# Crossing the moving columns of the split products, storing every second partition, and a new order of work from step 32 on

## The chip, the cores and the metric

The kernel runs on one core of a Trainium2 chip. A core has TensorE (PE, products of matrices), VectorE (DVE), ScalarE (ACT), GpSimd (POOL) and SyncE (SP, which here issues the transfers). Each works through its own list of instructions in order, and they wait for one another by semaphores. Operands lie in SBUF, on 128 partitions; products land in PSUM. The metric is the time on the device in microseconds (us), as a median over timed runs.

## What is computed

A retention layer (attention with a decay in place of the softmax) is followed by a feed-forward layer whose activation is a quotient of polynomials. From the reference, cut to what matters:

```python
scores = scale * np.matmul(q, k.transpose(0, 1, 3, 2))      # 8 x 8 heads, 576 x 64
ret = scores * Dmat[None, :, :, :]                          # Dmat = gamma ** (i - j), lower triangle
x = np.matmul(ret, v)                                       # as tokens: 4608 x 512
h = x @ w_in                                                # 512 x 2048
P = a[0] + a[1] * h + a[2] * h2 + a[3] * h3
Q = 1.0 + np.abs(b[0]) * np.abs(h) + np.abs(b[1]) * h2
g = P / (Q + 1e-06)
return (g @ w_out).astype(np.float32)                       # 2048 x 512
```

## The kernel before

The tokens are worked on in 9 blocks of 512 (`b`), and the 2048 inner columns in 16 slices of 128 (`f`). One step is one pair (b, f), 144 steps in all. The feed-forward part of a step is:

- `gemm1`: the first product, h = w_in slice x tokens, 128 partitions of inner columns by 512 tokens. To keep precision in the fast format fp32r, both factors are split into a rounded part and a rest (`xhi`, `xlo`; `w[:, 0]`, `w[:, 1]`), and three products are added up: 4 pieces of 128 x 3 = 12 products that each stream 512 columns of x.
- `ffn_p`, `ffn_p2`, `ffn_va`, `ffn_v`, `ffn_r`, `ffn_q`, `ffn_q3`: the activation on ScalarE and VectorE. ScalarE makes p and u from `h` (a2 + a3 h and |h|), later v from u, and the reciprocal of v as a logarithm and an exponential, both written into u. VectorE does `p*h`, `p2`, `v*u`, and after the reciprocal `p*u`, `v*u+..` and the last product p. `ffn_r`, `ffn_q` and `ffn_q3` of a step run one step later.
- `ffn_hi`, `ffn_lo`: the split of the result into `g[:, 0]` and `g[:, 1]`, two steps later.
- `gemm2`: the second product, three or four steps later. For each quarter t of the block (128 tokens), three products stream the 512 columns of w_out's slice and add to `acc`; 12 products a step. With the block's last slice, `acc` is copied to `o` and stored.

In the first part of the program, four slices of w_out aren't split yet when they are wanted; there `gemm2` takes one product in plain fp32 with the tile `held` (called `plain[f]` in the code), four a step, 16 in all.

The retention part is done in units of 128 tokens. A `visit` on PE takes 64x64 products for one unit's outputs (`ps`) and the next unit's scores and state (`y`, `ps`); `decay`, `add`, `keep_hi`, `keep_lo` and others bring them through VectorE, ScalarE and GpSimd. From step 30 on a visit comes every fourth step, the last at step 126.

The order of work within a step is written by hand: `run` goes through a list of names. Steps 0 to 31 have lists of their own (`FIRST..`, `MID`, `DENSE..`); all steps from 32 on use `REST`, and the last ones without a first product use `END`. The list sets the order on each engine, since every instruction is kept in program order. Transfers are all issued by SP, in the order in which the code comes to them: weights early, one unit's q, k and v after each visit, and the stores.

The tiles u and v have two buffers each, p three, and the tile `h` in PSUM two (one of which a visit takes for `y`).

Of the kernel before, what the change touches and what calls it, by code (L numbers as in the profile page):

```python
# [12 lines left out]
F32 = mybir.dt.float32  # L13
# [4 lines left out]
AF = mybir.ActivationFunctionType  # L18
ALU = mybir.AluOpType
PSUM = bass.MemoryType.PSUM  # L20

P = 128
B, H, S, D = 8, 8, 576, 64
NT = B * S
DM = H * D
DFF = 2048
NPAIR = H // 2
NU = NT // P
NB = NT // 512
NF = DFF // P  # L30
# [19 lines left out]
DENSE = "scale_q gemm1 visit decay ffn_p split0 ffn_hi split1 ffn_va ffn_r gemm2 ffn_lo keep_hi ffn_v ffn_p2 split2 split3 scale_v ffn_q ffn_q3 decay1 add keep_lo fade".split()  # L50
DENSE_ALONE = "gemm1 ffn_r ffn_p visit decay decay1 ffn_p2 ffn_q keep_hi split2 ffn_va add scale_v ffn_hi split3 ffn_v fade scale_q gemm2 split0 ffn_lo keep_lo ffn_q3 split1".split()
REST = (
    "gemm1 ffn_p visit ffn_p2 ffn_hi decay keep_hi ffn_lo decay1 add fade keep_lo scale_q scale_v ffn_va ffn_v gemm2 ffn_r"
    " ffn_q ffn_q3"
).split()
END = "ffn_r ffn_hi gemm2 ffn_lo ffn_q ffn_q3".split()

# [31 lines left out]
def retention_ffn(ctx: ExitStack, tc: tile.TileContext, qkv, w_in, w_out, consts, masks, out):  # L89
# [10 lines left out]
    nc = tc.nc  # L100
# [6 lines left out]
    cnv = ctx.enter_context(tc.tile_pool(name="cnv", bufs=4))  # L107
# [8 lines left out]
    pe, act, dve, pool = (InOrder(tc, e) for e in (nc.tensor, nc.scalar, nc.vector, nc.gpsimd))  # L116
# [43 lines left out]
    plain, held = {}, []  # L160
# [309 lines left out]
    part = []  # L470
    spare = {}

    def gemm1(b, f):
        xhi, xlo = xs[b]
        w = parts[0, f]
        h = hs[b, f] = ps_h.tile([P, 512], F32, tag="h", name=f"h{b}_{f}")
        for c in range(NPAIR):
            cs = slice(c * P, (c + 1) * P)
            for k, (j, x) in enumerate(((0, xhi), (0, xlo), (1, xhi))):
                pe.matmul(  # L480
                    h, w[:, j, cs], x[:, c, :], start=(c == 0 and k == 0), stop=(c == NPAIR - 1 and k == 2)
                )

    def ffn_p(b, f):
# [56 lines left out]
    def is_plain(b, f):  # L541
        return at[b, f] < half and str(f) in PLAIN
# [17 lines left out]
    def acc_of(b, t):  # L560
        return accs[b][2][:, 0, :] if b == NB - 1 and t == 3 else accs[b][t // 2][:, t % 2, :]

    def gemm2(b, f, first, last):
        if first:
            accs[b] = [ps_acc.tile([P, 2, DM], F32, tag="acc", name=f"acc{b}_{f}_{t}") for t in range(2)]
            if b == NB - 1:
                accs[b].append(ps_at.tile([P, 2, DM], F32, tag="at", name=f"acc{b}_{f}_2"))
        g = gs.pop((b, f))
        if is_plain(b, f):
            for t in range(4):  # L570
                pe.matmul(acc_of(b, t), g[:, t * P : (t + 1) * P], plain[f], start=first, stop=last)
            return
        w = parts[1, f]
        for t in range(4):
            ts = slice(t * P, (t + 1) * P)
            acc = acc_of(b, t)
            for k, (i, j) in enumerate(((0, 0), (0, 1), (1, 0))):
                pe.matmul(acc, g[:, i, ts], w[:, j, :], start=(first and k == 0), stop=(last and k == 2))
        if not last:
            return  # L580
        if b == NB - 1:
            for t in range(4):
                r0 = b * 512 + t * P
                o = cnv.tile([P, DM], F32, tag="c", name=f"o{b}_{t}")
                if t == 1:
                    dve.tensor_scalar(o, acc_of(b, t), -1.0, None, ALU.mult)
                else:
                    act.activation(o, acc_of(b, t), AF.Copy, scale=-1.0)
                nc.sync.dma_start(out[r0 : r0 + P, :], o)
            return  # L590
        for t, acc in enumerate(accs.pop(b)):
            r0 = b * 512 + t * 256
            rows = out[r0 : r0 + 256, :].rearrange("(t p) d -> p t d", p=P)
            if b == 1:
                for j in range(2):
                    o = cnv.tile([P, DM], F32, tag="c", name=f"o{b}_{t}_{j}")
                    act.activation(o, acc[:, j, :], AF.Copy, scale=-1.0)
                    nc.sync.dma_start(rows[:, j, :], o)
                continue
            if b == 0 and f == NF - 1:  # L600
                o = part[t]
                dve.scalar_tensor_tensor(o, acc, -1.0, o, ALU.mult, ALU.add)
            else:
                o = op.tile([P, 2, DM], F32, tag=f"o{t}", name=f"o{b}_{t}_{f}")
                act.activation(o, acc, AF.Copy, scale=-1.0)
            if f < NF - 1:
                part.append(o)
            else:
                nc.sync.dma_start(rows, o)

# [1 line left out]
    first = half + NF  # L614
# [81 lines left out]
    def products(i):  # L696
        nonlocal done
        while done < len(steps) and i - done >= lag(i):
            gemm2(*steps[done])
            done += 1  # L700

    for i in range(len(steps) + lag(len(steps))):
# [4 lines left out]
        if i in VISITS:  # L707
            a, k = VISITS[i]
# [63 lines left out]
```

## Time and profile before

| what | value |
|---|---|
| time, median of 3 runs | 894.04 us (893.99 to 895.55) |
| span of the profiled execution | 891.7 us |
| median less the span | 2.3 us |
| PE busy | 879.0 us, 99% |
| VectorE busy | 792.2 us, 89% |
| ScalarE busy | 674.3 us, 76% |
| GpSimd busy | 124.6 us, 14% |

The span runs from the first to the last instruction of one execution. The time of a run is a little longer, as it holds what lies around the span. A busy share is an average over the whole span, so it does not say which engine is waited for in a given stretch.

### The profile page before, as it was taken

The page shows a single profiled execution, that of the slowest core. Times are in us where ns is not written, and L with a number is a line of the kernel's source. Part 1 is how long each engine was busy: PE and PEld are TensorE (multiplying, and loading weights), DVE is VectorE, ACT ScalarE, POOL GpSimd, SP SyncE. Part 2 cuts the span into 40 slices and gives each one's busy share as a digit, 9 for nine tenths or more (in the row PEclk, how much of TensorE's full clock was granted, in tenths as well). Part 3 has the DMA queues.
Part 4 walks back from the last instruction along what each step waited for, and adds up shares of the span by engine and source line. Part 5 has one row for each costly group of instructions (what it writes and reads, how often), then busy time and mean ns, then how long its engine had stood idle before and what let it go on. Part 6 is the DMA issues. An engine that isn't in the chain of part 4 may idle for free.

```text
span 891.7 us, 18668 instructions
## 1 busy us (share of the span) xinstructions
PE 879.0 (99%) x7574; PEld 721.0 (81%) x7574; DVE 792.2 (89%) x1222; ACT 674.3 (76%) x1239; POOL 124.6 (14%) x107
## 2 busy tenths in 40 slices
PE   8899999999999999999999999999999999999998
PEld 6667888888888888888888888888888888888886
DVE  5999999998899888898999988888888989888895
ACT  4889998986677787777777787778777787667774
POOL 3424325421101100010111110111000111000000
PEclk9999999999999999999999999999999999999999
DMA  9993000141211112011211131112111021001001
GB/s 343 344 381 134 1 1 1 49 143 49 96 48 49 49 49 77 28 40 48 96 48 49 48 96 49 48 49 96 48 37 31 31 95 49 1 1 47 1 1 47
DMA packets 20454, 64.55 MB, mean 72 GB/s; under 512 B 2192, under 2 KB 2320, under 8 KB 20368
## 3 DMA queue, kind: packets, MB, share of 16 engines
q1 hardware_dynamic: 20368, 63.36, 20.2%
q8 instruction: 59, 0.97, 0.4%
q14 instruction: 27, 0.22, 0.1%
HBM read 53.91 MB, written 9.44 MB: 71 GB/s over the span
## 4 chain that ended last, share of the span: by engine, by line
PE 91%; DVE 5%; DMA 2%; ACT 1%; issue 1%; SPq 0%; DVEq 0%
PE acc L85 43%; PE h L85 41%; PE ps L85 4%; PE y L85 2%; DVE p L85 2%; DMA bits<-in_w_out 2%; PE psNone L85 1%; DVE v L85 1%; DMA qk<-in_qkv 1%; DVE qk L85 0%; DVE xlo L85 0%; DVE kv L85 0%; DVE c L85 0%; ACT o L85 0%; PE ps_None L85 0%
## 5 line engine op out<-in xcount | busy, mean ns | idle before, releaser
L85 PE MATMUL acc<-w,g 128*128 128x512 f32 x1584 | 384.3, 392 | 0.6 <-ACT o L85 0.3
L85 PE MATMUL h<-xhi,w 128*128 128x512 f32 x1152 | 378.9, 390 | 0.7 <-DVE kv L85 0.7
L85 PEld LDWEIGHTS acc<-w,g 128*128 128x128 f32 x1584 | 294.9, 188 | 63.6 <-ACT o L85 0.7
L85 PEld LDWEIGHTS h<-xhi,w 128*128 128x128 f32 x1152 | 216.3, 188 | 47.1 <-ACT u L85 1.0
L85 PE MATMUL h<-xlo,w 128*128 128x512 f32 x576 | 224.2, 389 | 0.1
L85 ACT ACTIVATE p<-h,const_sb 128x512 f32<-128x512 f32 x144 | 111.7, 776 | 127.8 <-PE h L85 123.6
L85 DVE SCALAR_TENSOR_TENSOR p<-p,const_sb,u 128x512 f32<-128x512 f32 x131 | 117.7, 899 | 15.6 <-ACT u L85 15.6
L85 PEld LDWEIGHTS h<-xlo,w 128*128 128x128 f32 x576 | 108.1, 188 | 23.4 <-issue 0.7
L85 DVE TENSOR_TENSOR p<-p,h 128x512 f32<-128x512 f32 x144 | 98.8, 686 | 28.1 <-ACT u L85 27.8
L85 DVE TENSOR_TENSOR v<-v,u 128x512 f32<-128x512 f32 x131 | 96.0, 733 | 24.8 <-ACT v L85 24.8
L85 ACT ACTIVATE u<-h 128x512 f32<-128x512 f32 x131 | 77.9, 594 | 48.0 <-DVE v L85 46.5
L85 DVE SCALAR_TENSOR_TENSOR p<-p,const_sb,h 128x512 f32<-128x512 f32 x144 | 107.6, 748 | 4.8
L85 ACT ACTIVATE v<-u,absb 128x512 f32<-128x512 f32 x129 | 103.9, 806 | 0.3 <-DVE p L85 0.2
L85 DVE SCALAR_TENSOR_TENSOR p<-v,p 128x512 f32<-128x512 f32 x140 | 97.5, 697 | 4.1
L85 DVE SCALAR_TENSOR_TENSOR v<-v,u 128x512 f32<-128x512 f32 x131 | 91.7, 700 | 0.0
L85 ACT ACTIVATE g<-p 128x512 fp32r<-128x512 f32 x132 | 83.3, 631 | 8.3 <-DVE p L85 3.4
L85 POOL TENSOR_TENSOR S<-S,const_sb 128x256 f32<-128x256 f32 x32 | 21.1, 659 | 472.6 <-DVE S L85 470.0
L85 ACT ACTIVATE u<-u 128x512 f32<-128x512 f32 x131 | 82.9, 633 | 4.2
L85 ACT ACTIVATE u<-v 128x512 f32<-128x512 f32 x131 | 81.3, 621 | 1.5 <-DVE v L85 1.5
L85 DVE TENSOR_TENSOR g<-p,g 128x512 fp32r<-128x512 f32 x115 | 78.7, 684 | 1.4 <-ACT g L85 1.4
L85 ACT ACTIVATE kv<-kv,const_sb 128x64 f32<-128x64 f32 x232 | 58.4, 339 | 4.8 <-DMA kv<-in_qkv 4.8
L85 POOL TENSOR_TENSOR qk<-qk,const_sb 128x512 f32<-128x512 f32 x31 | 48.4, 1562 | 47.5 <-DMA qk<-in_qkv 47.2
(93 smaller groups left out, 691.5 us busy)
## 6 DMA issues: line engine op xcount, KB each, us to landing
qk<-in_qkv SPq DMA_DIRECT2D x36, 512.0 KB, 4.0
kv<-in_qkv SPq DMA_DIRECT2D x32, 512.0 KB, 5.4
bits<-in_w_in SPq DMA_DIRECT2D x16, 512.0 KB, 9.5
bits<-in_w_out SPq DMA_DIRECT2D x16, 512.0 KB, 7.7
out<-o SPq DMA_DIRECT2D x14, 512.0 KB, 4.4
out<-o SPq DMA_DIRECT2D x8, 256.0 KB, 2.7
kv<-in_qkv SPq DMA_DIRECT2D x4, 256.0 KB, 6.8
const_sb<-in_consts SPq DMA_DIRECT2D x1, 265.0 KB, 3.1
```

The lines of the kernel that those rows point to most:

```text
L85: return lambda *a, **k: self.tc.keep_in_program_order(method(*a, **k))
```

## The change

All split products read their moving operand through `crossed`: column 0 of the first half, column 0 of the second half, column 1 of the first half and so on. The order of the 512 streamed columns is thereby changed, so the columns of `h`, `g` and the sums stand for other tokens: partition p of a sum's quarter t is token a x 256 + t x 64 + p // 2 with a = p % 2. Each store is therefore cut in two, one for the even and one for the odd partitions (`o[a::2]`). The columns of w_out are put in the opposite order on the host, so that the output's columns come out as they were; the `held` products read theirs crossed too. The list `REST` is new. A few lines of the diff that only change a tile's shape are cut.

```diff
 REST = (
-    "gemm1 ffn_p visit ffn_p2 ffn_hi decay keep_hi ffn_lo decay1 add fade keep_lo scale_q scale_v ffn_va ffn_v gemm2 ffn_r"
-    " ffn_q ffn_q3"
+    "gemm1 visit decay ffn_p scale_q decay1 ffn_p2 ffn_hi ffn_r ffn_va scale_v keep_hi ffn_lo ffn_q keep_lo add"
+    " ffn_q3 fade gemm2 ffn_v"
 ).split()
...
+    def crossed(x):
+        return x.rearrange("p (a n) -> p n a", a=2)
+
...
-                    h, w[:, j, cs], x[:, c, :], start=(c == 0 and k == 0), stop=(c == NPAIR - 1 and k == 2)
+                    h, w[:, j, cs], crossed(x[:, c, :]), start=(c == 0 and k == 0), stop=(c == NPAIR - 1 and k == 2)
...
-                pe.matmul(acc_of(b, t), g[:, t * P : (t + 1) * P], plain[f], start=first, stop=last)
+                pe.matmul(acc_of(b, t), g[:, t * P : (t + 1) * P], crossed(plain[f]), start=first, stop=last)
...
-                pe.matmul(acc, g[:, i, ts], w[:, j, :], start=(first and k == 0), stop=(last and k == 2))
+                pe.matmul(acc, g[:, i, ts], crossed(w[:, j, :]), start=(first and k == 0), stop=(last and k == 2))
...
-                nc.sync.dma_start(out[r0 : r0 + P, :], o)
+                store(b, t, o)
...
-                nc.sync.dma_start(rows, o)
+                store(b, 2 * t, o)
+
+    def store(b, t, o):
+
+        n = o.shape[1]
+        for a in range(2):
+            r0 = b * 512 + a * 256 + t * D
+            nc.sync.dma_start(out[r0 : r0 + n * D, :].rearrange("(t m) d -> m t d", m=D), o[a::2])
...
+    w_out = moe_w_out.reshape(DFF, DM // 2, 2).transpose(0, 2, 1)
...
-        "w_out": np.ascontiguousarray(moe_w_out).view(np.int64).reshape(NF, P, DM),
+        "w_out": np.ascontiguousarray(w_out).view(np.int64).reshape(NF, P, DM),
```

The order of the rows on PE and GpSimd is the same before and after, apart from the numbers in the names. The next two pairs show VectorE and ScalarE in one visit step from 32 on; the first number in a name is the slice f, the last one only tells buffers apart.

VectorE before, from slice 6's `p*h` (first row) to slice 5's last product; `qk`, `kv`, `S` and `xlo` are the visit's rows:

```order
L85 TENSOR_TENSOR p_6_3964<-p_6_3964,h_6_3949 128x512
L85 SCALAR_TENSOR_TENSOR p_6_3964<-p_6_3964,const_sb,h_6_3949 128x512
L85 TENSOR_TENSOR qk_3772<-y_3969,mask_sb 128x256
L85 COPY kv_3774<-y_3969 128x256
L85 TENSOR_TENSOR g_4_4041<-p_4_3871,g_4_4041 128x512
L85 TENSOR_TENSOR qk_3772<-ps_18_3968,mask_sb 128x256
L85 TENSOR_TENSOR S_4048<-kv_3774,ps_18_3968 128x256
L85 TENSOR_TENSOR xlo_3782<-ps_18_3968,xhi_3781 128x4x128
L85 TENSOR_TENSOR v_6_3963<-v_6_3963,u_6_3962 128x512
L85 SCALAR_TENSOR_TENSOR p_5_3913<-p_5_3913,const_sb,u_5_3911 128x512
L85 SCALAR_TENSOR_TENSOR v_5_3912<-v_5_3912,u_5_3911 128x512
L85 SCALAR_TENSOR_TENSOR p_5_3913<-v_5_3912,p_5_3913 128x512
```

VectorE after, the same step:

```order
L85 TENSOR_TENSOR qk_3772<-y_3971,mask_sb 128x256
L85 COPY kv_3774<-y_3971 128x256
L85 TENSOR_TENSOR p_6_4046<-p_6_4046,h_6_3957 128x512
L85 TENSOR_TENSOR qk_3772<-ps_18_3970,mask_sb 128x256
L85 SCALAR_TENSOR_TENSOR p_6_4046<-p_6_4046,const_sb,h_6_3957 128x512
L85 TENSOR_TENSOR g_4_4052<-p_4_3879,g_4_4052 128x512
L85 SCALAR_TENSOR_TENSOR p_5_3921<-p_5_3921,const_sb,u_5_3919 128x512
L85 SCALAR_TENSOR_TENSOR v_5_3920<-v_5_3920,u_5_3919 128x512
L85 TENSOR_TENSOR xlo_3792<-ps_18_3970,xhi_3791 128x4x128
L85 TENSOR_TENSOR S_4062<-kv_3774,ps_18_3970 128x256
L85 SCALAR_TENSOR_TENSOR p_5_3921<-v_5_3920,p_5_3921 128x512
L85 TENSOR_TENSOR v_6_4045<-v_6_4045,u_6_4044 128x512
```

The step's own `v*u` (v_6) has moved behind the two readers of the previous slice's reciprocal (u_5) and is now last; the rows that read `y` have moved ahead of `p*h`.

ScalarE before, the same step; u_5<-v_5 and u_5<-u_5 are the logarithm and the exponential:

```order
L85 ACTIVATE p_6_3964<-h_6_3949,const_sb 128x512
L85 ACTIVATE u_6_3962<-h_6_3949 128x512
L85 ACTIVATE g_4_4041<-p_4_3871 128x512
L85 ACTIVATE xhi_3781<-ps_18_3968 128x4x128
L85 ACTIVATE v_6_3963<-u_6_3962,absb 128x512
L85 ACTIVATE u_5_3911<-v_5_3912 128x512
L85 ACTIVATE u_5_3911<-u_5_3911 128x512
```

ScalarE after, from slice 4's g (the rows p_6 and u_6 stand ahead of it as before):

```order
L85 ACTIVATE g_4_4052<-p_4_3879 128x512
L85 ACTIVATE u_5_3919<-v_5_3920 128x512
L85 ACTIVATE u_5_3919<-u_5_3919 128x512
L85 ACTIVATE v_6_4045<-u_6_4044,absb 128x512
L85 ACTIVATE xhi_3791<-ps_18_3970 128x4x128
```

The logarithm and exponential of slice 5 have moved ahead of slice 6's v and of the visit's `xhi`.

SP's last rows before, the stores of the last block:

```order
L609 DMA out<-o_0_15_8771 128x2x512
L609 DMA out<-o_1_15_8774 128x2x512
L589 DMA out<-o_0_9374 128x512
L589 DMA out<-o_1_9377 128x512
L589 DMA out<-o_2_9380 128x512
L589 DMA out<-o_3_9383 128x512
```

And after:

```order
L616 DMA out<-o_0_15_8791 64x2x512 x2
L616 DMA out<-o_1_15_8795 64x2x512 x2
L616 DMA out<-o_0_9392 64x512 x2
L616 DMA out<-o_1_9396 64x512 x2
L616 DMA out<-o_2_9400 64x512 x2
L616 DMA out<-o_3_9404 64x512 x2
```

Each store has become two of half the partitions, issued one after the other in the same place.

## Rows read from the trace of the kernel before

**Rows 1.** The page: span, busy time of PE, clock in 40 slices.

```profile
span 891.7 us, 18668 instructions
...
PE 879.0 (99%) x7574; PEld 721.0 (81%) x7574; DVE 792.2 (89%) x1222; ACT 674.3 (76%) x1239; POOL 124.6 (14%) x107
...
PEclk9999999999999999999999999999999999999999
```

**Rows 2.** Chain that ended last, 860 to 892 us: start, length, what.

```profile
860.18 2.72 PE h L85 x12
...
873.78 13.61 PE acc L85 x60
```

**Rows 3.** Stretches: length, busy PE, PEld, DVE, ACT, POOL, clock, DMA share, GB/s.

```profile
25.61:216.94 191.33, 188.59 (x1697) 149.43 (x1693) 183.63 (x292) 168.57 (x313) 66.96 (x52) 1.00 0.33 121
75.68:94.72 19.04, 19.04 (x86) 15.77 (x84) 18.93 (x31) 17.36 (x31) 7.48 (x6) 1.00 0.02 9
385.10:409.12 24.02, 24.02 (x226) 19.90 (x224) 21.80 (x34) 17.68 (x34) 2.22 (x2) 1.00 0.14 45
768.59:792.02 23.43, 23.31 (x162) 19.06 (x160) 18.99 (x30) 15.05 (x26) 0.00 (x0) 1.00 0.00 1
792.02:813.78 21.76, 21.76 (x98) 18.02 (x96) 17.64 (x28) 15.50 (x25) 0.00 (x0) 1.00 0.13 49
```

**Rows 4.** Groups by shape, PE: count, busy us, mean ns.

```profile
L85 PE MATMUL acc<-w,g 128*128 128x512 f32 x1584 | 384.3, 392 | 0.6 <-ACT o L85 0.3 <-DVE o L85 0.3
L85 PE MATMUL h<-xhi,w 128*128 128x512 f32 x1152 | 378.9, 390 | 0.7 <-DVE kv L85 0.7
L85 PE MATMUL h<-xlo,w 128*128 128x512 f32 x576 | 224.2, 389 | 0.1
...
L85 PE MATMUL acc<-w,spare 128*128 128x512 f32 x96 | 22.7, 389 | 0.0
```

**Rows 5.** Timeline of PE at 59 us: start, length of the run of eight.

```profile
58.95 3.59 PE L85 MATMUL acc<-held,g 128*128 128x512 f32 x8
```

**Rows 6.** The tile `held`, weight loads (PEld) and products: shortest, median and longest ns.

```profile
L85 PEld LDWEIGHTS acc<-held,g x32: 186/190/190, 40.9 to 69.3; 128*128 128x128 f32 x32
L85 PE MATMUL acc<-held,g x32: 590/592/697, 40.9 to 69.8; 128*128 128x512 f32 x32
```

**Rows 7.** Groups of VectorE and ScalarE, 216.94 to 862.60 us (645.66 us).

```profile
L85 ACT ACTIVATE p<-h,const_sb 128x512 f32<-128x512 f32 x109 | 84.7, 777 | 112.2 <-PE h L85 110.7 <-DVE v L85 1.4
L85 DVE SCALAR_TENSOR_TENSOR p<-p,const_sb,h 128x512 f32<-128x512 f32 x110 | 82.3, 748 | 3.9
L85 DVE TENSOR_TENSOR v<-v,u 128x512 f32<-128x512 f32 x110 | 77.7, 707 | 24.6 <-ACT v L85 24.6
L85 DVE SCALAR_TENSOR_TENSOR v<-v,u 128x512 f32<-128x512 f32 x110 | 77.3, 703 | 0.0
...
L85 DVE TENSOR_TENSOR p<-p,h 128x512 f32<-128x512 f32 x109 | 75.0, 688 | 23.2 <-ACT u L85 23.0
L85 DVE TENSOR_TENSOR g<-p,g 128x512 fp32r<-128x512 f32 x105 | 71.8, 684 | 0.0
L85 ACT ACTIVATE u<-u 128x512 f32<-128x512 f32 x109 | 69.0, 633 | 3.5
L85 ACT ACTIVATE u<-v 128x512 f32<-128x512 f32 x109 | 67.6, 620 | 0.0
L85 ACT ACTIVATE g<-p 128x512 fp32r<-128x512 f32 x105 | 66.4, 633 | 4.6
L85 ACT ACTIVATE u<-h 128x512 f32<-128x512 f32 x109 | 64.9, 596 | 47.0 <-DVE v L85 45.6
```

**Rows 8.** The output tensor: the last four stores' issues, ns.

```profile
L589 SPq DMA_DIRECT2D out<-o x4: 344/378/413, 886.7 to 888.3; - x4
```

**Rows 9.** What SP waited for: us in total, times, longest.

```profile
SPq L377 <- PE ps L85: 633.4, 59, 98.8
```

**Rows 10.** The page's transfers: KB each, median us from issue to landing.

```profile
qk<-in_qkv SPq DMA_DIRECT2D x36, 512.0 KB, 4.0
```

## What I expect, and why

> **What bounds the kernel now.** I read the page first: in a span of 891.7 us TensorE (PE) is busy 99%, and its granted clock is at the upper level, 2.4 GHz, in every slice [rows 1]. Then the chain that ended last: near its end it shows PE's big products in unbroken runs, 12 in 2.72 us and 60 in 13.61 us [rows 2]. That is 226.7 ns from one product to the next. A product streams 512 columns, and at 2.4 GHz one column a cycle would take 213.3 ns; 13.4 ns of each product are something else. The groups by shape count 1584 + 1152 + 576 + 96 = 3408 such split products [rows 4], 772.6 us at this pace, 87% of the span.
>
> The table of stretches says where PE alone sets the pace. A period of four steps with one visit takes 24.02 us and PE is busy in all of it; four steps without a visit take 21.76 us, which is 96 x 226.7 ns to the last digit [rows 3]. In the early part it is different: from 75.68 to 94.72 VectorE (DVE) works 18.93 of 19.04 us, as full as PE [rows 3].
>
> One other kind of product in this trace streams 512 columns of four-byte numbers: those with `held`, kept in plain fp32. The code asks for 16 and the records show 32, so each is two passes. Eight passes in a row take 3.59 us, the last one's 592 ns among them [rows 5, 6], so one follows the other after (3.59 - 0.592) / 7 = 0.4283 us. That is 1024 cycles at 2.4 GHz (426.7 ns) and 1.6 ns more: a column every second cycle, with next to nothing on top. The same bytes lose 1.6 ns at half the pace and 13.4 ns at the full pace.
>
> **The change: crossed columns.** The products, their count and PE's order stay; only the addresses of the moving columns change: 0, 256, 1, 257 and so on, two places 1 KB apart, each read at half the pace. No row shows such a stream, so I bound it. From below 213.3 + 1.6 = 214.9 ns a product, if the loss is that one place doesn't deliver a column in every cycle; from above 428.3 ns, a column every second cycle, the pace of the `held` row. Between them lies 226.7, no effect. I take 215.2 ns, a saving of 11.5 ns, near the lower end: the loss goes with the full pace of one stream, `held` reads one place at half pace and loses almost nothing, and each of the two places is now read at just that pace. Waiting for weights it is not: `held` has loads of the same 128 x 128 shape, 190 ns each, without the loss [rows 6], and 190 ns is less than the product that a load lies under.
>
> The Trainium skill, "TensorE: Matmul & The Clock Gate", section "Wait — 56ns, not 53.3ns?", gives 215.7 ns from one warm 512-column product to the next. The split products here don't reach it (226.7 ns); by its figure the saving would be 11.0 ns, an estimate, and the sum some 1.4 us smaller.
>
> **What of it reaches the end.** From 216.94 us on (step 32) there are 112 x 12 first products and 115 x 12 second ones, which run three steps behind: 2724 x 11.5 ns = 31.3 us. A period falls from 24.02 to 24.02 - 96 x 0.0115 = 22.92 us. VectorE has 21.80 us of work in it [rows 3], so it still fits, with 1.1 us to spare where it had 2.2. Some of what it waits for now is only PE's pace, handed on by ScalarE as `u` (23.0 us ahead of `p*h` in this stretch); but 24.6 us are waits for ScalarE's `v` [rows 7], 24.6 / (645.66 / 24.02) = 0.9 us a period, and ScalarE's `u` waits 45.6 us for VectorE's `v` [rows 7]: the two hand work back and forth.
>
> *The new order* changes ScalarE's and VectorE's rows from step 32 on. Before, a step's `v*u` stands on VectorE ahead of the previous step's two readers of the reciprocal, which queue behind its wait; now it is the last row of the step, and ScalarE does logarithm and exponential ahead of `v`. By durations, from `h` ready: ScalarE's p 0.78, u 0.60, g 0.63, logarithm 0.62, exponential 0.63 end at 3.26 us; VectorE, behind `u` (1.38), does `p*h`, `p2` and `g`, 0.69 + 0.75 + 0.68, until 3.50 us [rows 7], so the reciprocal is there when it is wanted. The buffer that the next `u` needs is free after two more rows, 3.50 + 0.75 + 0.70 = 4.95 us, ahead of the next `h` at 24 x 0.2152 = 5.16 us. So the 0.9 us go. What remains is unevenness: each visit puts some 21.80 - 17.64 = 4.2 us more work for VectorE into one step of four [rows 3], against 24.02 - 21.76 = 2.26 us for PE; VectorE falls behind by some 1.2 us and has three steps with 0.7 us to spare each to make it up, while PE has a second buffer for `h`. For the 24 visits I allow 0.12 us each, 2.9 us (none at all, or the 0.9 us kept without cover, 21.80 + 0.9 = 22.7, would still be under 22.92). 31.3 - 2.9 = 28.4 us.
>
> *Before step 32* there are 684 products, 7.9 us at most; VectorE leaves 191.33 - 183.63 = 7.7 us idle there in all, and stretches like 75.68 to 94.72, where it leaves 0.11 us, give nothing [rows 3]. I take a quarter of the 7.9, 1.9 us.
>
> *Stores.* Each becomes two of 64 partitions on SP's queue, 22 issues to 44, at 378 ns the median one of the last four [rows 8]. In the middle SP waits 633 us on the visits alone [rows 9], and the loads behind a store land in 4.0 us [rows 10] and are scaled three steps, some 16 us, later; that cover makes the extra issues free, and without it they would cost 22 x 0.378 = 8.3 us. At the end nothing covers them: the second half of the last store is issued 0.38 us later, with half the bytes in each: +0.3 us.
>
> *Sum.* On the profiled execution 891.7 - 28.4 - 1.9 + 0.3 = 861.7 us. The median of the timed runs, 894.04, lies 2.3 us above that span, so 864 us.
>
> **The rivals.** *VectorE takes up what PE gives.* If all its 2.2 us of waits in a period stay, because ScalarE and VectorE hand work back and forth as before, a period with a visit stays at 24.0, and only the steps without visits, from 768.59 us on [rows 3], gain (some 516 products, 5.9 us) with the 1.9 us early: 886. For it: VectorE is busy 91% of a period. Against it: the timing of the new order above. A loss of which half is removed (220.9 ns) gives much the same: 894 - 15 - 1 = 878.
>
> *The excess belongs to the product, not to the addresses*: a fixed turn between products that shows only when the stream is short. Nothing excludes it, as all split products have one length. Then only the order and the tail move: 893 to 895, since PE is full anyway.
>
> *The other side: jumping is dearer than running on.* One mechanism: a column whose neighbour isn't read right after it needs a fetch of its own, and the stream waits for it. At worst a product goes to 428.3 ns: 3408 x 201.6 ns = 687 us more, 1581 us. It decides from 0.5 ns a product on (1.8 us over 3408). For it: no moving operand in this trace jumps, so nothing shows that a jump is free. Against it: at half the pace each place has the time that it has in `held`.
>
> The Trainium skill, "SBUF — State Buffer", section "Door 1: The DMA port swizzle (why `[64,N]` ≈ `[32,N]`)", speaks for this rival: lines of 16 bytes, of which at least two accesses in a row are wanted, and a penalty for each step to a new line. By it a product makes 512 line changes where it makes 128 now; if the 11.8 ns are the price of 128, four times that gives 262 ns a product and about 1013 us, an estimate. No row of this trace shows it.
>
> **How the numbers follow.** Loss gone and VectorE keeping up: 0.50, 857 to 873 us. Loss gone in part, or VectorE in the way: 0.14, 873 to 892. No effect: 0.13, 892.3 to 895.8 (0.2%, 1.8 us, is about what a measurement of this kernel can tell from no change). Slower: 0.23, nearly all of it above 900, since any real price is paid 3408 times. The prediction is the first case, 864, and its own range 857 to 873. The whole range, 856 to 898, holds the first three cases and leaves out the slower one. Faster 0.64, same 0.13, slower 0.23.
>
> **What would show it.** Right: twelve split products in 2.58 us in the chain, periods of 22.9 to 23.1 us, VectorE busy 93% or more in them, `v` no longer waiting for ScalarE, 0.3 us more behind the last product. Wrong: a pace of 226.7 (the excess is the product's own), one above it (jumps cost), or the new pace with periods still near 24 (VectorE). The prediction stands or falls with the pace of one product, on which the trace before has only the `held` row to say.

## The result and the profile after

The changed kernel takes 873.31 us (median of 4 runs, 873.01 to 874.14) against 894.01: a ratio of 0.9766, 95% interval 0.9752 to 0.978. That is 20.7 us less where 30 were forecast. The profiled execution has a span of 871.7 us, 1.6 less than the median (2.3 before).

The page first, its span and its busy times [rows 1 for before]:

```profile
span 871.7 us, 18740 instructions
PE 851.0 (98%) x7574; PEld 727.6 (83%) x7574; DVE 774.6 (89%) x1222; ACT 664.8 (76%) x1239; POOL 131.5 (15%) x107
```

PE has lost 28.0 us of busy time, the span 20.0. So 8 us of what the products gave went elsewhere. The chain that ended last shows the pace itself and what stands behind the last first product (start, length, what):

```profile
842.73 2.59 PE h L85 x12
845.32 2.59 PE acc L85 x12
847.91 2.60 PE h L85 x12
...
861.10 0.64 ACT g L85
861.74 0.04 issue
861.78 0.70 PE acc L85 x2
862.50 2.44 PE acc L85 x10
864.95 0.02 issue
864.97 0.60 ACT o L85
```

Twelve products take 2.59 us where they took 2.72 [rows 2]: 215.9 ns each, 10.8 less. The stretches are steps 0 to 31, a part of them, one period with a visit, four steps without one, and step 32 to the end of the last first product (length, busy PE, PEld, DVE, ACT, POOL, clock, DMA share, GB/s):

```profile
28.00:222.93 194.93, 185.89 (x1696) 149.76 (x1693) 187.63 (x292) 174.93 (x313) 66.60 (x52) 1.00 0.32 114
98.49:121.11 22.62, 20.98 (x97) 18.06 (x96) 22.09 (x34) 21.52 (x35) 6.97 (x6) 1.00 0.00 1
383.93:406.87 22.94, 22.94 (x225) 20.02 (x224) 20.53 (x34) 16.82 (x34) 2.60 (x2) 1.00 0.14 47
772.64:793.36 20.72, 20.72 (x97) 18.14 (x96) 18.17 (x29) 16.09 (x26) 0.00 (x0) 1.00 0.08 32
...
222.93:850.34 627.41, 626.65 (x5497) 546.36 (x5496) 562.40 (x894) 468.47 (x887) 54.46 (x42) 1.00 0.15 50
```

A period has gone from 24.02 to 22.94 us and PE is still busy in all of it [rows 3]. Steps 0 to 31 have got longer, 191.33 to 194.93 us, with VectorE's busy time up from 183.63 to 187.63. In four parts, with the borders at the first product of step 0, at that of step 32, and where the product behind the last first one starts (850.34 us):

| part | before | after | moved | forecast |
|---|---|---|---|---|
| ahead of step 0 | 25.61 | 28.00 | +2.4 | 0 |
| steps 0 to 31 | 191.33 | 194.93 | +3.6 | -1.9 |
| step 32 to the last first product | 656.7 | 627.4 | -29.3 | -28.4 |
| behind it | 18.1 | 21.4 | +3.3 | +0.3 |
| span | 891.7 | 871.7 | -20.0 | -30.0 |

The large part came out about as forecast; the three small ones all went the wrong way. The groups of VectorE and ScalarE from 222.93 to 842.73 us answer to [rows 7] (count, busy us, mean ns, idle before):

```profile
L85 ACT ACTIVATE p<-h,const_sb 128x512 f32<-128x512 f32 x110 | 85.2, 775 | 150.9 <-PE h L85 148.1 <-DVE g L85 2.7
...
L85 DVE TENSOR_TENSOR v<-v,u 128x512 f32<-128x512 f32 x110 | 83.1, 756 | 0.0
...
L85 DVE TENSOR_TENSOR p<-p,h 128x512 f32<-128x512 f32 x110 | 75.4, 685 | 36.9 <-ACT u L85 35.0
...
L85 ACT ACTIVATE u<-h 128x512 f32<-128x512 f32 x110 | 64.3, 585 | 1.0 <-DVE v L85 0.9
```

The wait for `v` (24.6 us) is gone, and so is `u`'s wait for VectorE's `v` (45.6, now 0.9). What VectorE still waits for, `u`, is PE's pace handed on: ahead of its p, the row that comes before `u`, ScalarE waits 148.1 us for PE's `h`.

For steps 0 to 31 two tiles tell more. `held`, the plain fp32 products [rows 6], and `bits`, the weight words that ScalarE and VectorE bring into fp32 (shortest, median and longest ns):

```profile
L85 PE MATMUL acc<-held,g x32: 701/703/804, 43.6 to 74.6; 128*128 128x512 f32 x32
...
L85 ACT ACTIVATE bits<-bits x32: 654/870/980, 20.6 to 175.7; 128x512 int32<-128x512 uint32 x32
L85 ACT ACTIVATE c<-bits x28: 655/862/910, 20.0 to 175.2; 128x512 f32<-128x512 f32 x28
L85 DVE SCALAR_TENSOR_TENSOR c<-c,bits x28: 679/835/1955, 21.7 to 178.9; 128x512 int32<-128x512 int32 x28
```

The kernel before has for the last three:

```profile
L85 ACT ACTIVATE bits<-bits x32: 648/668/691, 18.5 to 168.0; 128x512 int32<-128x512 uint32 x32
L85 ACT ACTIVATE c<-bits x28: 649/661/689, 17.9 to 167.4; 128x512 f32<-128x512 f32 x28
L85 DVE SCALAR_TENSOR_TENSOR c<-c,bits x28: 678/684/1782, 19.6 to 171.1; 128x512 int32<-128x512 int32 x28
```

Nobody touched these rows, and their medians rose by 150 to 200 ns. All read every second four-byte word of a tile; rows that read neighbours, like VectorE's g<-p with 684, kept their length in these steps. The `held` passes rose from 592 to 703 ns. Both are taken up in the experiments.

At the end the timeline of SP has the last stores (start, length of all, the line, count), after and before:

```profile
864.29 4.98 SPq L616 DMA_DIRECT2D out<-o  x8
```

```profile
886.68 2.08 SPq L589 DMA_DIRECT2D out<-o  x4
```

One issue of a store of every second partition takes 608 ns at the median, not 378 [rows 8]. From the end of PE's last product to the end of the span it is now 871.7 - 864.94 = 6.8 us, before 4.3 (PE ended at 873.78 + 13.61 = 887.39): 2.5 of the 3.3 us. The other 0.8 lie between the last first product and PE's last second one, 14.6 us against 13.8: before, PE ran its 60 last products without a break [rows 2]; now the chain there goes through the last step's activation and its `g`, which didn't get faster.

Ahead of step 0, PE's timeline (start, length, what, count):

```profile
8.68 1.12 PE L85 MATMUL unread<-whole_sb,qk 128*128 128x128 f32 x4
...
11.53 1.12 PE L85 MATMUL unread<-whole_sb,qk 128*128 128x128 f32 x4
...
16.08 0.66 PE L85 MATMUL unread<-whole_sb,qk 128*128 128x128 f32 x4
```

Four such products take 1.12 us twice and then 0.66; before, those at 10.03 us took 0.66 already. The change moves nothing there. In the profiled executions of the experiments step 0 began at 25.39 to 26.56 us in eight and at 28.96 and 29.23 in two (x_crossed and early_less). In x_crossed the granted clock is 0.50, the lower of its two levels (1.2 GHz), near 13 us, behind a wait of PE of 1.59 us at 9.34. In early_less such products take 1.12 us at 9.17 and 12.28 us and 0.66 at 17.32, and there the granted clock shows it, in the windows view from 8 to 18 us:

```profile
8.00:18.00 10.00, 7.81 (x78) 6.21 (x78) 4.19 (x8) 3.69 (x11) 2.70 (x3) 0.66 1.03 411
```

That is 0.66 of 2.4 GHz as a mean, between the lower and the upper level, behind PE's wait of 1.83 us at 9.17. For the changed kernel's own profile the view reads 1.00 in that window, but its trace holds no record of the clock ahead of 14.05 us, and the view counts such time as full; in the other eleven profiles the record begins between 3.9 and 6.6 us. The products fit the lower level up to there: 1.12 us at 11.53 us, 0.66 at 16.08. So a granted clock that rose late in this execution is the likely cause, though no record of the lower level shows it. The 2.4 us belong to the execution; how much of them is in the medians stays open. This bears on every comparison with this profile: a part of the difference of two spans can lie ahead of step 0, so the parts of the span are given where they matter.

### The profile page after: what moved, and what is told of

It is laid out like the page before. It is cut to its first block, busy times and chain, and to the rows that moved or that the text cites. A ratio compares the mean times of both kernels' runs of the same rounds, so it can differ in the third digit from the quotient of the medians.

```text
span 871.7 us, 18740 instructions
## 1 busy us (share of the span) xinstructions
PE 851.0 (98%) x7574; PEld 727.6 (83%) x7574; DVE 774.6 (89%) x1222; ACT 664.8 (76%) x1239; POOL 131.5 (15%) x107
## 4 chain that ended last, share of the span: by engine, by line
PE 81%; DVE 11%; ACT 4%; issue 2%; DMA 1%; POOL 0%; SPq 0%; ACTq 0%; DVEq 0%; POOLq 0%
PE acc L85 37%; PE h L85 36%; DVE p L85 5%; PE ps L85 4%; DVE v L85 3%; PE y L85 2%; DVE c L85 1%; PE psNone L85 1%; ACT free_at L85 1%; ACT g L85 1%; DMA qk<-in_qkv 1%; DVE qk L85 0%; ACT bits L85 0%; ACT c L85 0%; ACT u L85 0%
## 5 line engine op out<-in xcount | busy, mean ns | idle before, releaser
L85 PE MATMUL h<-xhi,w 128*128 128x512 f32 x1152 | 367.8, 381 | 3.9 <-DVE p L85 3.2
L85 PE MATMUL acc<-w,g 128*128 128x512 f32 x1584 | 367.8, 381 | 3.4 <-ACT o L85 1.6
L85 PE MATMUL h<-xlo,w 128*128 128x512 f32 x576 | 218.4, 379 | 0.1
L85 DVE TENSOR_TENSOR v<-v,u 128x512 f32<-128x512 f32 x131 | 101.4, 774 | 0.2 <-ACT v L85 0.2
L85 DVE SCALAR_TENSOR_TENSOR p<-p,const_sb,u 128x512 f32<-128x512 f32 x131 | 99.3, 758 | 1.2 <-ACT u L85 1.2
L85 POOL TENSOR_TENSOR S<-S,const_sb 128x256 f32<-128x256 f32 x32 | 27.1, 848 | 454.9 <-DVE S L85 454.9
L85 DVE SCALAR_TENSOR_TENSOR v<-v,u 128x512 f32<-128x512 f32 x131 | 89.4, 683 | 0.0
```

The source lines that it names most:

```text
L85: return lambda *a, **k: self.tc.keep_in_program_order(method(*a, **k))
```

## Experiments

The medians of before beside these runs are 893.7 to 893.9 us. Ratios are against before, with 95% intervals.

**cross_only: the crossed columns with the old order.**

```diff
 REST = (
-    "gemm1 visit decay ffn_p scale_q decay1 ffn_p2 ffn_hi ffn_r ffn_va scale_v keep_hi ffn_lo ffn_q keep_lo add"
-    " ffn_q3 fade gemm2 ffn_v"
+    "gemm1 ffn_p visit ffn_p2 ffn_hi decay keep_hi ffn_lo decay1 add fade keep_lo scale_q scale_v ffn_va ffn_v gemm2 ffn_r"
+    " ffn_q ffn_q3"
 ).split()
```

> The change with the old list REST from step 32 on. Theory: the pace of one product does all the work and the order little, because even with the 0.9 us of waits for ScalarE's v kept in a period VectorE needs 21.8 + 0.9 = 22.7 us, less than PE's 22.94; periods stay at 22.9 to 23.1 us and the time at 872 to 876 us. Rival: the old order hands work back and forth between ScalarE and VectorE and can't follow the shorter step; periods of 23.3 to 24.0 us, 24 of them, 882 to 893 us.

884.51 us (883.53 to 885.35), 0.989 (0.9874 to 0.9907): 11.2 us slower than the change. In the profiled executions the part from step 32 to the last first product is 13.7 us longer. Its window of one period, and its waits from 246 to 760 us (us in total, times, longest):

```profile
410.32:433.96 23.64, 23.34 (x225) 19.86 (x224) 21.45 (x34) 19.31 (x35) 2.30 (x2) 1.00 0.25 89
```

```profile
ACT u L85 <- DVE v L85: 85.8, 85, 2.3
DVE v L85 <- ACT v L85: 27.1, 22, 1.2
...
PEld h L85 <- DVE p L85: 14.2, 20, 1.0
...
PE h L85 <- DVE p L85: 6.0, 18, 0.6
```

The old order holds a period at 23.64 us, and PE now waits for VectorE's `p`, the reader that gives `h` free, though VectorE is busy for only 21.45 of it. The two engines hand work back and forth, and that chain binds before either is full.

**order_only: the kernel before with the new order.** The same list the other way round:

```diff
 REST = (
-    "gemm1 ffn_p visit ffn_p2 ffn_hi decay keep_hi ffn_lo decay1 add fade keep_lo scale_q scale_v ffn_va ffn_v gemm2 ffn_r"
-    " ffn_q ffn_q3"
+    "gemm1 visit decay ffn_p scale_q decay1 ffn_p2 ffn_hi ffn_r ffn_va scale_v keep_hi ffn_lo ffn_q keep_lo add"
+    " ffn_q3 fade gemm2 ffn_v"
 ).split()
```

> The kernel before with nothing but the new list REST. Theory: PE is full at 226.7 ns a product in either order, so 893 to 895 us, no change. Rival: the order is worth something by itself, in the periods around step 32 and at the end; under 892 us.

895.21 us (894.58 to 898.04), 1.0015 (1.0003 to 1.0027). One period:

```profile
385.40:409.40 24.00, 24.00 (x225) 19.89 (x224) 20.52 (x34) 16.84 (x34) 2.61 (x2) 1.00 0.14 45
```

VectorE's wait for ScalarE's `v` (23.6 us from 246 to 760 us before) is gone, its rows are shorter (20.52 us against 21.80), and the time doesn't fall, since PE was full; by the interval it is up to 0.27% longer. Crossing alone brings 9.2 us, the order alone nothing, both together 20.7: the order is worth 11.2 us, but only at the new pace.

**held_natural: the `held` products read their columns in a row again**, because the rows that write `held` put them there:

```diff
             cf = plain[k[1]] = held[i % 2][:, i // 2, :]
+            cf = cf.rearrange("p (n a) -> p a n", a=2)
...
-        dve.scalar_tensor_tensor(c, c, 3, low, ALU.logical_shift_left, ALU.bitwise_or)
+        dve.scalar_tensor_tensor(c, c, 3, fit(low), ALU.logical_shift_left, ALU.bitwise_or)
...
-                pe.matmul(acc_of(b, t), g[:, t * P : (t + 1) * P], crossed(plain[f]), start=first, stop=last)
+                pe.matmul(acc_of(b, t), g[:, t * P : (t + 1) * P], plain[f], start=first, stop=last)
```

> The change, with the four plain fp32 slices (held) laid out so that their products stream contiguous columns; their writers on ScalarE and VectorE step over every second column instead. Theory: crossed streaming made each of the 32 fp32 passes about 111 ns longer (703 for 592 ns in the median), and they lie on the path in steps 4 to 8: 32 x 0.111 = 3.5 us less, 869 to 871 us. Rival: transfers and VectorE bind there anyway, the saved time turns into waiting, 872.5 to 874 us.

870.85 us (870.35 to 873.76), 0.9748 (0.9729 to 0.9767), 2.5 us better than the change at the median. The tile `held`:

```profile
L85 PE MATMUL acc<-held,g x32: 592/592/697, 40.9 to 69.7; 128*128 128x512 f32 x32
...
L85 DVE SCALAR_TENSOR_TENSOR held<-held,bits x4: 679/932/961, 34.5 to 56.5; 128x512 int32<-128x512 int32 x4
L85 ACT ACTIVATE w<-held x4: 842/867/908, 77.2 to 93.4; 128x512 fp32r<-128x512 f32 x4
```

The passes are back at 592 ns, 32 x 0.111 = 3.5 us less of PE; a part of it went into rows that now step over every second column (w<-held was 620, VectorE's was 818 in the change). Hardly any of it arrives. Steps 0 to 31 in this profile:

```profile
25.53:219.81 194.28, 183.62 (x1697) 149.94 (x1694) 187.32 (x292) 176.50 (x313) 67.64 (x52) 1.00 0.33 120
```

PE is busy for 2.3 us less than with the change (185.89), but the stretch is only 0.65 us shorter (194.93): the rest has become waiting, as the rival said, though the median lies in the theory's range. The other 2.5 us between the two spans (868.5 and 871.7) lie ahead of step 0, which began at 25.53 us and not at 28.00. So the 2.5 us at the median are not shown to come from the `held` passes.

**x_crossed: `xhi` and `xlo` written in crossed places**, so that the sums stand in their natural partitions and each store is one again:

```diff
-        act.activation(x_part(x_of(n // 4)[0], n), sums_of(n), AF.Copy)
+        act.activation(x_part(x_of(n // 4)[0], n), by_two(sums_of(n)), AF.Copy)
...
-        for a in range(2):
-            r0 = b * 512 + a * 256 + t * D
-            nc.sync.dma_start(out[r0 : r0 + n * D, :].rearrange("(t m) d -> m t d", m=D), o[a::2])
+        r0 = b * 512 + t * P
+        nc.sync.dma_start(out[r0 : r0 + n * P, :].rearrange("(t p) d -> p t d", p=P), o)
```

> The change, but xhi and xlo are written with their columns already crossed, so that the crossed stream gives tokens in their own order and every store is whole again (22 of 128 partitions in place of 44 of every second one). Theory: the last four stores took 4.98 us of issuing in place of 2.08 us, and this is the end of the program: 2.5 to 3 us less, 870 to 871 us. Rival: the scattered writes of xhi and xlo take longer on ScalarE and VectorE (0.58 and 0.68 us each now), 36 of each, and the gain is lost where these engines are full; 872 to 876 us.

873.27 us (872.64 to 875.82), 0.9774 (0.9755 to 0.9792): no gain. The four last stores are back at 2.08 us, but the writers of the two tiles pay:

```profile
L85 ACT ACTIVATE xhi<-ps x30: 1081/1088/1134, 34.7 to 749.0; 128x512 fp32r<-128x512 f32 x30
```

```profile
L85 DVE TENSOR_TENSOR xlo<-ps,xhi x30: 1060/1078/1124, 36.4 to 751.1; 128x512 fp32r<-128x512 f32 x30
```

They were 575 and 681 ns in the change. A write that jumps 1 KB after each element takes half as long again or more. In the profiled execution the time behind PE's last product is 2.3 us shorter than with the change, and steps 0 to 31 take 198.34 us, 3.4 longer. Not all of that is the writers': near 47 us a stretch of it has a granted clock of 0.50.

**ways: other patterns for the moving columns**, one for each slice of the second product, the first product in a row:

```diff
+WAYS = (
+    [("whole", 0)] + [("apart", n) for n in (2, 4, 8, 16, 64, 128, 256)] + [("pieces", n) for n in (2, 4, 8, 16, 64)]
+    + [("cut", 256), ("whole", 0), ("whole", 0)]
+)
...
+        if kind == "apart":
+            return x.rearrange("p (a n) -> p n a", a=n)
+        if kind == "pieces":
+            return x.rearrange("p (a n c) -> p n a c", a=2, c=n)
```

> The kernel before with the new order; the first product streams contiguous columns, the second one streams a different pattern in each of the 16 slices f: contiguous; one column from each of 2, 4, 8, 16, 64, 128, 256 places in turn (1 KB, 512, 256, 128, 32, 16, 8 bytes apart); pieces of 2, 4, 8, 16, 64 columns from the two halves in turn; two products of 256 contiguous columns in place of one of 512; contiguous twice. Theory of the prediction (one place doesn't deliver a column in each cycle, two places at half the pace do): 215 to 216 ns for the columns from 2, 4, 8 and 16 places and for pieces of 2, near 226.7 for pieces of 64 and for 8 bytes apart, where only one place is read at a time. Rival, any stream that leaves the row of neighbours is free of the excess: 216 for every pattern but contiguous. The cut product: 2 x 120 = 240 ns if the 13.4 ns are the product's own, 226.7 to 229 if they go with the columns. Plain fp32 passes of slices 0 to 3 (contiguous, 2, 4, 8 places): 428 ns for the first, some 540 for the others if a jump costs there.

1051.29 us, of a single run. PE's timeline has one run of twelve for each slice; here a product cut into two of 256 columns in a row, and one of 512 columns in a row:

```profile
483.18 3.04 PE L89 MATMUL acc<-w,g 128*128 128x256 f32 x24
488.80 2.88 PE L89 MATMUL acc<-w,g 128*128 128x512 f32 x12
```

The pace from start to start, medians in ns:

| moving columns | ns |
|---|---|
| in a row | 227 |
| two halves in turn | 216 |
| 4 places in turn | 283 |
| 8, 16, 64, 128, 256 places in turn | 553, 433, 431, 460, 452 |
| two halves, pieces of 2, 4, 8, 16, 64 columns | 340, 251, 242, 240, 227 |
| in a row, cut in two of 256 | 120 each |
| fp32 pass: in a row, two halves, 4 places | 429, 540, 873 |

My reason falls by two rows. A product of 256 columns in a row takes 120 ns, 13.3 more than its 106.7 of columns (256 at 2.4 GHz): the excess is paid once a product, whatever its length, not by the column. And more places, each read more slowly still, are far worse, not better. "Jumping is dearer" holds from 4 places on and for pieces, and not for two places. What two places in turn take away is the fixed turn of a product.

**ways2: how far apart the two places must be, and whether the turn is the weights'.** Here slices 7 to 10 stream other columns than the reference's, and slices 11 to 13 leave out a part of the sums; the time counts alone.

```diff
+WAYS = (
+    [("apart", n) for n in (128, 64, 32, 16, 8, 4, 2)] + [("far", n) for n in (260, 288, 384, 512)]
+    + [("few", 64), ("few_crossed", 64), ("few", 32), ("cut", 256), ("whole", 0)]
+)
...
+            return w[:, j, :].rearrange("p (b a n) -> p b n a", a=2, n=n)
```

> As ways, with other patterns in the second product of the 16 slices: columns from two places in turn that lie 512, 256, 128, 64, 32, 16 and 8 bytes apart (slices 0 to 6); two places 1040, 1152, 1536 and 2048 bytes apart (7 to 10); contiguous with 64 columns of weights loaded (11), 1 KB apart with 64 (12), contiguous with 32 (13); 1 KB apart cut into two products of 256 columns (14); contiguous (15). Slices 7 to 10 stream columns of other places than they should, 11 to 13 leave out the sums of half or three quarters of the tokens. In ways the excess of 13.3 ns was the product's own (120 ns for 256 columns), and two places 1 KB apart had 216 ns where 4 places 512 bytes apart had 283. Theory, two places whatever their distance: 216 ns for all of slices 0 to 10. Rival, the distance matters: 216 only from 1 KB on, 250 to 450 below. Theory on the excess, the load of 128 weights takes the stream's turns: some 221 ns with 64 weights and 219 with 32; rival, a turn at the start of each product: 226.7 with any number of weights. Cut in two, 1 KB apart: 109 ns each if what is left (2.6 ns) is a product's own, as the 120 for contiguous.

889.99 us, of a single run. PE's timeline, with runs of 64 columns of weights crossed, 32 columns of weights in a row, and halves cut into two of 256:

```profile
501.91 2.75 PE L89 MATMUL acc<-w,g 128*64 128x512 f32 x12
...
507.25 2.94 PE L89 MATMUL acc<-w,g 128*32 128x512 f32 x12
...
512.79 2.84 PE L89 MATMUL acc<-w,g 128*128 128x256 f32 x24
```

Two places 512, 256, 128, 64, 32 and 16 bytes apart: 216 ns each; 8 bytes apart: 227, as in a row; 1040, 1152, 1536 and 2048 bytes: 216. With a quarter of the weight columns a product in a row takes 231 ns, so the turn isn't the weight load's. Cut in two, crossed products take 112 ns and those in a row 120. The border lies between 8 and 16 bytes: two places gain if they are at least 16 bytes apart.

**early_plain: steps 0 to 31 stream in a row again**, `held` too. The copies to `o` put the columns back, and the stores of these two blocks are whole again.

```diff
-                    h, w[:, j, cs], crossed(x[:, c, :]), start=(c == 0 and k == 0), stop=(c == NPAIR - 1 and k == 2)
+                    h, w[:, j, cs], crossed(x[:, c, :]) if b > 1 else x[:, c, :], start=(c == 0 and k == 0), stop=(c == NPAIR - 1 and k == 2)
...
-                pe.matmul(acc_of(b, t), g[:, t * P : (t + 1) * P], crossed(plain[f]), start=first, stop=last)
+                pe.matmul(acc_of(b, t), g[:, t * P : (t + 1) * P], plain[f], start=first, stop=last)
...
-                pe.matmul(acc, g[:, i, ts], crossed(w[:, j, :]), start=(first and k == 0), stop=(last and k == 2))
+                pe.matmul(acc, g[:, i, ts], crossed(w[:, j, :]) if b > 1 else w[:, j, :], start=(first and k == 0), stop=(last and k == 2))
...
```

> The change with blocks 0 and 1 (steps 0 to 31) left contiguous in both products and in the held products; their sums are put back in order by the copies to o, their stores are whole. In the change, rows of VectorE and ScalarE that read every second word (the splitting of the weights) last longer than before: c<-c,bits 835 for 684 ns, c<-bits some 865 for 662, bits<-bits some 915 for 667. Theory: the crossed stream of PE makes them longer, and VectorE and ScalarE are full in these steps. Then these rows return to 684, 662 and 667 ns, steps 0 to 31 take 191 to 192 us in place of 194.9, although every split product in them is 10.8 ns longer, and the time is 869 to 871 us. Rival: the rows got longer by meeting GpSimd's at other times; they stay long here, the products' 768 x 10.8 ns = 8 us come on top, 876 us or more.

869.65 us (868.34 to 870.34), 0.9724 (0.9707 to 0.974): 3.7 us better at the median, although 720 split products take 10.8 ns more each. In the profiled executions steps 0 to 31 take 192.10 us, 2.8 less than with the change; 1.4 us lie ahead of step 0, and from step 32 on it loses 0.7. The tile `bits`:

```profile
L85 ACT ACTIVATE bits<-bits x32: 650/667/699, 19.1 to 170.2; 128x512 int32<-128x512 uint32 x32
L85 ACT ACTIVATE c<-bits x28: 649/660/697, 18.6 to 169.6; 128x512 f32<-128x512 f32 x28
L85 DVE SCALAR_TENSOR_TENSOR c<-c,bits x28: 676/683/1789, 20.3 to 173.3; 128x512 int32<-128x512 int32 x28
```

The rows of ScalarE and VectorE are back at the lengths of before, by an edit that touches only PE's addresses, the copies to `o` and those stores. So PE's two-place stream is what lengthens rows that read every second word.

**two_queues: three of the last eight stores on ScalarE's queue.**

```diff
-                store(b, t, o)
+                ends.append(o)
+                store(b, t, o, (0, 1) if t == 0 else (0,))
+            for t in range(1, 4):
+                store(b, t, ends[t], (1,), nc.scalar)
...
```

> The change, with three of the last eight store halves issued on ScalarE's queue behind its last copy. Theory: the eight issues on SP, 4.98 us in all and one after the other, set the end; five on SP end near 3.1 us after the first, three on ScalarE 1.8 us after its last copy, so the end comes 1.7 to 2.2 us earlier, 871 to 871.6 us. Rival: the transfers of the halves, not the issuing, set the end; 873 us as it is.

870.22 us (869.07 to 871.18), 0.9731 (0.9714 to 0.9749), 3.1 us better than the change. SP's timeline at the end:

```profile
863.75 3.08 SPq L620 DMA_DIRECT2D out<-o  x5
```

The issues on SP take 4.98 - 3.08 = 1.9 us less, and in the profiled executions the time behind PE's last product falls by the same 1.9 us. The rest of the gain doesn't lie there: step 0 began 1.8 us earlier than in the change's profile (26.18 us), and steps 0 to 31 took 1.3 us longer, with a granted clock of 0.51 in a stretch near 43 us. So 1.9 of the 3.1 us are shown to be the stores'.

**early_two: the last two together.** It is the edits of both, no line more.

> early_plain and two_queues together. Theory: the two costs lie in different places (steps 0 to 31, and the end), so they add: 3.6 + 2 us, 867 to 869.5 us. Rival: what is won early is lost again where the old pace meets the new order at step 32; 870 us or more.

866.85 us (866.33 to 867.3), 0.9696 (0.9679 to 0.9713). Steps 0 to 31:

```profile
25.39:216.86 191.47, 188.58 (x1697) 149.43 (x1693) 183.65 (x292) 168.82 (x315) 66.41 (x52) 1.00 0.33 122
```

That is as before the change (191.33) and 3.5 us less than with it. At the medians 873.31 - 866.85 = 6.5 us are near the 3.7 and the 3.1 added up. Between the two profiled executions 7.1 us lie: 3.5 in steps 0 to 31 and 1.8 behind PE's last product, which are the edits', 2.6 ahead of step 0, which neither edit touches, and 0.7 lost from step 32 on.

**early_less: as early_two, with the second product of steps 24 to 31 crossed.**

```diff
-                pe.matmul(acc, g[:, i, ts], crossed(w[:, j, :]) if b > 1 else w[:, j, :], start=(first and k == 0), stop=(last and k == 2))
+                pe.matmul(acc, g[:, i, ts], crossed(w[:, j, :]) if b > 1 or b == 0 and f >= half else w[:, j, :], start=(first and k == 0), stop=(last and k == 2))
```

> early_two with the second product of steps 24 to 31 (block 0, second half) crossed again, its sums then need no putting back. Theory: PE sets the pace in steps 28 to 31 (VectorE leaves some 3 us there), so about 48 x 10.8 ns = 0.5 us, at most 96 x 10.8 = 1.0 us less than early_two's 866.85: 865.8 to 866.4 us. Rival: the last rows of weight splitting in these steps get longer again under the crossed stream; 866.8 us or more.

865.66 us (5 runs, 865.57 to 868.84), 0.9691 (0.9678 to 0.9705). It has the lowest median of all, 873.31 - 865.66 = 7.7 us below the change, but its interval overlaps that of early_two: that this last edit gains anything isn't shown by the medians. The profiles point to a gain: against early_two's, steps 0 to 31 are 0.6 us shorter and the part from step 32 to the last first product 0.7, while step 0 began 3.8 us later. That is one execution of each.

## Why the prediction was right, and where it was not

**The change: crossed columns.** The size was right, 215.9 ns for 215.2, a saving of 10.8 ns for 11.5. The reason was wrong, and so it was luck that the value came out at the lower end of the bounds of 214.9 to 428.3 ns: four places, which the reason favours as much, take 283. I argued from `held`, which loses 1.6 ns at half the pace, that one place can't deliver a column in every cycle; ways shows 13.3 ns lost by a product of 256 columns as by one of 512 (226.7 - 213.3 = 13.4). `held`, crossed, was no free ride either: 429 ns a pass became 540. The rival "the excess belongs to the product, not to the addresses" was right about where the excess sits and wrong that addresses can't remove it. The Trainium skill, "TensorE: Matmul & The Clock Gate", section "Wait — 56ns, not 53.3ns?", has 215.7 ns for this length, and the trace now agrees with 215.9; with the columns in a row these products stood 11 ns above it.

**The other side.** Jumping is dearer from four places on (283 to 553 ns) and in pieces of 2 to 16 columns (240 to 340), so this rival was one pattern away. The Trainium skill, "SBUF — State Buffer", section "Door 1: The DMA port swizzle (why `[64,N]` ≈ `[32,N]`)", wants at least two accesses in a row in a 16-byte line. The runs agree with the size of the line, as the border lies between 8 and 16 bytes; they disagree for two places in turn, where each column is in another line than the one ahead of it and the product is faster, 216 against 227 ns. Nor do two accesses in a row in a line suffice: pieces of two columns take 340 ns.

**What of it reaches the end, and the new order.** -29.3 us for -28.4: 2724 x 10.8 ns = 29.4, so that all of it arrived and the 2.9 us that I allowed for uneven steps weren't needed. Two misses nearly cancel here, a saving that was 1.9 us too large and an allowance of 2.9. One sign did not come: VectorE busy 93% or more in a period. It is 89% (20.53 of 22.94 us), because I carried its 21.80 us over and the new order by itself shortens its rows (20.52 in order_only; VectorE's p<-p,const_sb,u from step 32 on has 745 ns there and 912 before). The reading of the new order held: the wait for `v` went from 24.6 us to nothing. One sentence in that step was wrong: that the 0.9 us of waits, kept, "would still be under 22.92". In cross_only the waits are kept and a period takes 23.64. Adding a wait to VectorE's busy time misses the chain through ScalarE, which lengthens when PE's pace no longer hides it. "VectorE takes up what PE gives" came near the truth in that kernel: 884.51 us where the rival said 886, though a period did fall, from 24.02 to 23.64 us.

**Before step 32** is the step that failed: +3.6 us for -1.9. I costed the change at PE alone and asked only whether VectorE leaves room. Two prices were missing. The `held` passes are dearer by 111 ns, 3.5 us of PE, but taking that away shortens these steps by only 0.65 us (held_natural). And rows of ScalarE and VectorE that read every second word get longer by 150 to 200 ns while PE streams from two places; where VectorE is full (22.09 of 22.62 us from 98.49 on), PE waits for it. early_plain takes both away, and its profile has 2.8 us less in these steps, early_two's 3.5: by subtraction most of it is the longer rows' (held_natural made a few rows dearer too, so the split is rough).

**Stores** had the right place and the wrong size: +0.3 for 2.5. I took the length of an issue from a store of all partitions, 378 ns, and one more of them; an issue over every second partition takes 608, and eight in a row on one queue add up. The cover in the middle held. The 0.8 us of activation behind the last first product were not in the sum at all.

**Ahead of step 0** nothing was forecast and 2.4 us appeared, in that one execution, most likely by a clock that rose late.

So 873.3 lies within the whole range and 0.3 us above the own range of the likeliest case: its mechanism from step 32 on was the one that came, and some 11 us (2.4 + 5.5 + 3.0) were lost against the forecast in the parts that I had counted at next to nothing.

## What to carry to other kernels

When an edit changes how one engine reads SBUF, look at the lengths of the rows of all the others in the stretch, not only at that engine's pace: here a gain of 10.8 ns a product came with 150 to 200 ns on rows that nobody had touched. Use such an edit where its engine binds and leave it out where another is full. An edit that does nothing alone (the order at the old pace) can be worth 11 us once another is in: ask of each engine what it waits for then. And before a difference of two profiles is put down to an edit, see in which part of the span it lies.

## What the runs showed of the hardware

- An fp32r product of columns in a row pays 13.3 ns beyond its columns at both lengths tried (227 ns for 512, 120 for 256), with 128, 64 or 32 weight columns (227, 229, 231). Two places in turn, at least 16 bytes apart, pay 2.6 for 512 (216 ns) and 5 for 256 (112). Why exactly two do this, and four or pieces of two columns the opposite, stays open.
- fp32 passes go the other way: 429 ns in a row, 540 from two places, 873 from four. The cause is open.
- While PE streams from two places, ScalarE's rows that read every second word go from 661 to 862 ns and from 668 to 870, VectorE's from 684 to 835; with PE in a row they are at the old lengths. In ways the same row of VectorE took 847 ns beside two halves and 681 beside four places, whose stream is slower (one row each). Separating the words in memory ahead of time was not tried.
- A write that jumps 1 KB after each element took 1088 ns for 575 on ScalarE and 1078 for 681 on VectorE.
- An issue of a store over every second of 128 partitions took 608 ns, over all of them 352 to 394 (medians of three groups).
